# An attention and spectral-mixing kernel: the first two output pairs take the last two chunks of modes from their sums in place of one

## The chip, the cores and the metric

The kernel runs on one core of a Trainium2 chip. The core has five engines that run side by side, each with an instruction queue of its own that is worked off in order: TensorE (PE in the profile, with its weight loads as PEld), VectorE (DVE), ScalarE (ACT), GpSimd (POOL) and SyncE (SP). In this kernel POOL and SP do little but issue transfers (DMAs), which sixteen DMA engines carry out. Matrix products land in PSUM[...]; everything else lies in SBUF, 128 partitions wide.

The metric is the device time of one execution in microseconds. The time of a kernel is the median of several executions.

## The reference

First causal attention with a bias that decays, for 8 batches and 8 heads, over 576 positions with 64 numbers each. Its output, with the heads side by side, is `x` (8 x 576 x 512). Then a spectral layer:

```python
X = np.fft.rfft(x, axis=1)                 # 64 modes are kept
Xr, Xi = real(X[:, :64]), imag(X[:, :64])
Yr = einsum('bmd,mde->bme', Xr, w_r) - einsum('bmd,mde->bme', Xi, w_i)
Yi = einsum('bmd,mde->bme', Xr, w_i) + einsum('bmd,mde->bme', Xi, w_r)
y = np.fft.irfft(Yr + 1j * Yi, n=576, axis=1)
u = x + y
return u + np.maximum(u @ w_ch, 0.0)
```

`w_r` and `w_i` are 64 x 512 x 512 in float32, 64 MiB each, and each number of them is used once for all batches.

## The kernel before

**Stages.** The loop over `n` (32 steps, up to about 340 us) does attention for two heads of one batch at a time, and the forward Fourier sums (`fft`). The 512 columns of `x` come in four groups `g` of 128; the modes come in eight chunks `c` of eight. `modes(g, c)` multiplies one chunk with the weights of one group: 16 matmuls in four lots `x` = 0 to 3, each with one weight tile of its own (real and imaginary part, even and odd modes). The sums over the groups are kept in `y_acc`; the last group, `g` = NG - 1, gives the finished chunk `yb` (128 rows: 16 of real and imaginary modes for each of 8 batches, by 512 columns, float16).

**Weights.** POOL issues the loads (`load`, L217), 512 KB into each tile, into a ring of tiles. The issue of a load waits until `modes` has read the tile that it replaces. The loads for the last chunk are all issued by the time chunk 5 of the last group has been multiplied.

**After a chunk.** `spread` (L465) issues from SP a transfer inside SBUF that sorts the 16 x 8 rows of `yb` so that rows 16c to 16c+15 of `yv[:, b, 0, :]` hold chunk c for batch b. `y_transposed` and `y_times_wch` form `v = yb @ w_ch` (a cast `v_sb` on DVE at the end, L630), and a second `spread` puts it into `yv[:, b, 1, :]`.

**Outputs.** `pairs` lists the output tiles two by two: pair 0 is positions 0 to 255 of batch 0, pair 1 positions 256 to 511 of batch 0. For each, `u` = x + G.y (`start_u` L678, then `add_y` with `which` = 0, L659) and `z` = x @ w_ch + G.(y @ w_ch) (`add_y` with `which` = 1), where G are the numbers of the inverse transform. Then `relu` and `finish` (L712) give the result, and SP sends it out (L714). For pairs 2 and on the product x @ w_ch was formed earlier and kept (`keep`); pairs 0 and 1 (`NPRE` = 2) take it straight from PSUM (`x_transposed` L590, `x_times_wch` L600).

**The first two pairs.** So that they need not wait for the last chunk to be sorted, `add_y` reads only the first `GK` = 112 rows of `yv` for them (chunks 0 to 6), and `add_last` (L668) adds chunk 7 from `yb` or `vb` directly. Its stationary operand `Gx_sb` holds the 16 rows of G for chunk 7, at every eighth partition, and zeros elsewhere, so that of the 128 rows of `yb` only those of batch 0 count. It is loaded whole, zeros included, by one transfer from SP (L561).

**Order.** The order of each engine's instructions is that of the program text (`manual_schedule`); waits are put in by the framework wherever a tile is written and read. TensorE's order at the end of the chunks, L731 to L748, is written out by hand: `x_transposed(0)`, `x_transposed(1)`, `x_times_wch(0)`, `modes(3, 6)`, `y_transposed`, `y_times_wch(6)`, `x_times_wch(1)`, `start_u(0)`, `add_y` of u for pair 0, then `modes(3, 7)`, in which the call `meanwhile` ahead of lot 3 (L438) does `add_y` of z for pairs 0 and 1. L750 to L773 then finish pairs 0 and 1, and the loop at L802 does the other sixteen.

**PSUM.** Two slots each for the pools `aux` (chunk sums, transposes, v), `u` and `z`.

Of the kernel before, what the change touches and what calls it, by code (L numbers as in the profile page):

```python
# [9 lines left out]
FP32 = mybir.dt.float32  # L10
FP16 = mybir.dt.float16
# [7 lines left out]
def kernel(  # L19
# [11 lines left out]
    nc = tc.nc  # L31
    B, H, S, D = q.shape
    NM = moe_w_r.shape[0]
    DM = H * D
    P = 128
# [4 lines left out]
    NG = DM // P  # L40
# [5 lines left out]
    MC = 8  # L46
    NCK = NM // MC
# [3 lines left out]
    NF = NT - 1  # L51
# [10 lines left out]
        axis=1,  # L62
# [11 lines left out]
    G_np = np.zeros((NM, 2, SP), dtype=np.float64)  # L74
    G_np[:, 0, :S] = cmv[:, None] * np.cos(ang.T)
    G_np[:, 1, :S] = -(cmv[:, None] * np.sin(ang.T))
    G_np = G_np.reshape(P, SP).astype(np.float16)
# [6 lines left out]
    d_Ff = nc.inline_tensor(Ff_np, name="c_Ffwd").ap()  # L84
    d_G = nc.inline_tensor(G_np, name="c_Ginv").ap()

    Gx_np = np.zeros((2 * MC, B, NF * P), dtype=np.float16)
    Gx_np[:, 0] = G_np[-2 * MC :, : NF * P]
    d_Gx = nc.inline_tensor(Gx_np.reshape(P, NF * P), name="c_Ginvx").ap()

    ctx.enter_context(tc.manual_schedule())
    gp = ctx.enter_context(tc.tile_pool(name="globals", bufs=1))
# [98 lines left out]
    def ring_of(k):  # L191
        if k < NE:
            return None
        return int(k < LW2 and (k - NE) % (WA + WB) >= WA)
# [33 lines left out]
    for n in range(N):  # L228
# [3 lines left out]
        while nt < min(w, len(wq)):  # L232
            i = ring_of(nt)
# [37 lines left out]
    with tc.tile_pool(name="cum_psum", bufs=1, space=PSUM) as cpsum:  # L271
# [5 lines left out]
            out=cum, data0=spos, data1=zer, initial=0.0, op0=ALU.add, op1=ALU.add  # L277
# [16 lines left out]
        for x in range(2):  # L294
            rows = slice(NL * x, NL * x + NL)
            nc.vector.tensor_copy(
                out=cumt4[rows, :], in_=cumt_sb[rows, NK, x::2]
# [132 lines left out]
    def modes(g, c, meanwhile=None):  # L430


        ps = auxpool.tile([P, DM], FP32, name="yp", tag="aux")
        for x in range(4):
            ri, par = divmod(x, 2)
            cols = xs[g % 2].rearrange("p k r b m -> p (k r b) m")
            c0 = (48, 16)[ri] - 16 * par
            if x == 3 and meanwhile:  # L438
                meanwhile()
            for cg in range(4):  # L440
                nc.tensor.matmul(  # L441
                    ps[32 * cg : 32 * cg + 32, :],
                    cols[:, c0 : c0 + 32, c * MC + 2 * cg + par],
                    wt[(g, c, ri, par)][:, cg, :],
                    start=(x == 0), stop=(x == 3),
                    tile_position=(0, 32 * cg), skip_group_check=True,
                )
        if g == 0:
            nc.vector.tensor_copy(out=y_acc[:, c, :], in_=ps)
        elif g < NG - 1:  # L450
            nc.vector.tensor_tensor(out=y_acc[:, c, :], in0=ps, in1=y_acc[:, c, :], op=ALU.add)
        else:
            yb = spool.tile([P, DM], FP16, name="y_sb", tag="y")
            for cols in halves if c == NCK - 1 else [slice(0, DM)]:
                nc.vector.tensor_tensor(
                    out=yb[:, cols], in0=ps[:, cols], in1=y_acc[:, c, cols], op=ALU.add
                )
            spread(c, 0, yb)
            return yb
# [3 lines left out]
    def spread(c, which, rows):  # L463

        nc.sync.dma_start(out=yv[16 * c : 16 * c + 16, :, which, :], in_=rows)  # L465
# [7 lines left out]
    NPRE = 2  # L473
# [45 lines left out]
    with tc.tile_pool(name="sc_psum", bufs=2, space=PSUM) as scpool, \  # L519
# [7 lines left out]
        for n in range(N):  # L527
# [9 lines left out]
            i = first_pairs[n - N + len(first_pairs)] if n >= N - len(first_pairs) else None  # L537
# [19 lines left out]

    finpool = ctx.enter_context(tc.tile_pool(name="fin_sb", bufs=1))
    yv = finpool.tile([P, B, 2, DM], FP16, name="yv")
    Gx_sb = finpool.tile([P, NF * P], FP16, name="Gx_sb")  # L560
    nc.sync.dma_start(out=Gx_sb, in_=d_Gx)  # L561
    upool = ctx.enter_context(tc.tile_pool(name="u_psum", bufs=2, space=PSUM))
    zpool = ctx.enter_context(tc.tile_pool(name="z_psum", bufs=2, space=PSUM))

# [13 lines left out]
    def parts(b, T):  # L578

        if T < NF:  # L580
            return [(slice(0, P), b, ident16h)]
        return [(slice(NL * i, NL * i + NL), b + i, ident16h[:NL, :NL]) for i in range(2)]

    def x_transposed(i):
        xts[i] = xt_sb[len(xts) % 2]
        for x, (b, T) in enumerate(pairs[i]):
            ps = upool.tile([P, DT, P], FP32, name="xt_ps", tag="u")
            for rows, bb, ident in parts(b, T):
                for dt in range(DT):
                    nc.tensor.matmul(  # L590
                        ps[:, dt, rows], x_all[: rows.stop - rows.start, dt, bb, T, :],
                        ident, start=True, stop=True, skip_group_check=True,
                    )
            nc.vector.tensor_copy(out=xts[i][:, x], in_=ps)

    def x_times_wch(i, last):
        zs[i] = z = zpool.tile([P, 2, DM], FP32, name="z_ps", tag="z")
        for x in range(2):
            for dt in range(DT):
                nc.tensor.matmul(  # L600
                    z[:, x, :], xts[i][:, x, dt, :], wch_sb[:, dt, :],
                    start=(dt == 0), stop=(last and dt == DT - 1), skip_group_check=True,
                )
# [11 lines left out]
    def y_transposed(yb):  # L615
        ps = auxpool.tile([P, DT, P], FP16, name="yt_ps", tag="aux")
        for dt in range(DT):
            nc.tensor.transpose(ps[:, dt, :], yb[:, bass.ts(dt, P)], ident16h)
        yt = spool.tile([P, DT, P], FP16, name="yt_sb", tag="yt")
        nc.scalar.copy(out=yt, in_=ps)  # L620
        return yt

    def y_times_wch(c, yt):
        vp = auxpool.tile([P, DM], FP32, name="v_ps", tag="aux")
        for dt in range(DT):
            nc.tensor.matmul(
                vp, yt[:, dt, :], wch_sb[:, dt, :], start=(dt == 0), stop=(dt == DT - 1)
            )
        vb = spool.tile([P, DM], FP16, name="v_sb", tag="v")
        nc.vector.tensor_copy(out=vb, in_=vp)  # L630
        spread(c, 1, vb)
        return vb
# [17 lines left out]
    order_z = list(late)  # L650
    TAKE = (3, 2, 2, 2, 1, 0)
    us, rs = {}, {}
    GK = P - 2 * MC

    def add_y(dst, i, which, rows=slice(0, P), start=False):

        for x, (b, T) in enumerate(pairs[i]):
            for r, bb, _ in parts(b, T):
                nc.tensor.matmul(  # L659
                    dst[x][r, :], G_sb[rows, bass.ds(T * P, r.stop - r.start)],  # L660
                    yv[rows, bb, which, :], start=start, stop=True, skip_group_check=True,
                    tile_position=(0, r.start),
                )

    def add_last(dst, i, yb, cols=slice(0, DM)):

        for x, (b, T) in enumerate(pairs[i]):
            nc.tensor.matmul(  # L668
                dst[x][:, cols], Gx_sb[:, bass.ts(T, P)], yb[:, cols],
                start=False, stop=True, skip_group_check=True,  # L670
            )

    def start_u(i):
        pool, tag = ((upool, "u"), (auxpool, "aux"))[i % 2]
        us[i] = [pool.tile([P, DM], FP32, name="u_ps", tag=tag) for x in range(2)]
        for x, (b, T) in enumerate(pairs[i]):
            for r, bb, ident in parts(b, T):
                nc.tensor.matmul(  # L678
                    us[i][x][r, :].rearrange("p (g d) -> p g d", d=P), ident,
                    x_all[: r.stop - r.start, :, bb, T, :],  # L680
                    start=True, stop=False, skip_group_check=True, tile_position=(0, r.start),
                )
# [35 lines left out]
    def z_of(i):  # L718
        return [zs[i][:, x, :] for x in range(2)]

    for c in range(NCK - 2):
        yb = modes(NG - 1, c)
        for x in range(TAKE[c] - 1):
            work()
        yt = y_transposed(yb)
        if TAKE[c]:
            work()
        y_times_wch(c, yt)
    work()
    assert not order_z and not ahead  # L730
    c = NCK - 2  # L731
    for i in range(NPRE):
        x_transposed(i)
    x_times_wch(0, False)
    yb = modes(NG - 1, c)
    yt = y_transposed(yb)
    y_times_wch(c, yt)
    x_times_wch(1, False)


    start_u(0)
    add_y(us[0], 0, 0, slice(0, GK))

    def first_sums():
        for i in range(NPRE):
            add_y(z_of(i), i, 1, slice(0, GK))

    yb = modes(NG - 1, NCK - 1, first_sums)  # L748

    yt = spool.tile([P, DT, P], FP16, name="yt_sb", tag="yt")  # L750
    for x in range(2):
        dts = slice(x * DT // 2, (x + 1) * DT // 2)
        ps = auxpool.tile([P, DT // 2, P], FP16, name="yt_ps", tag="aux")
        for dt in range(dts.start, dts.stop):
            nc.tensor.transpose(ps[:, dt - dts.start, :], yb[:, bass.ts(dt, P)], ident16h)
        nc.scalar.copy(out=yt[:, dts], in_=ps)
    add_last(us[0], 0, yb)
    vb = spool.tile([P, DM], FP16, name="v_sb", tag="v")
    for cols in halves:
# [7 lines left out]
    for i in range(NPRE):  # L767
        for cols in halves:
            add_last(z_of(i), i, vb, cols)
        relu(i, 2 - i)  # L770
    start_u(1)
    add_y(us[1], 1, 0, slice(0, GK))
    add_last(us[1], 1, yb)  # L773


# [65 lines left out]
```

The softmax here doesn't subtract the row's maximum and nothing guards it: scores larger than these inputs give would overflow.

## Time and profile before

| | |
|---|---|
| median of 10 runs | 463.58 us (461.79 to 464.46) |
| profiled execution | 463.75 us, of which 462.0 us are the span of the profile |
| busy in the span | PE 343.6 us (74%), DVE 233.5 (51%), ACT 219.0 (47%), POOL 182.9 (40%) |
| DMA | 95.16 MB, 206 GB/s on the mean |
| POOL's queue of transfers (the weights among them) | 81.81 MB |
| weight loads (L217) | 512 KB each |
| landing of the sixteen `yv` spreads (128 KB each) | 2.9 to 6.5 us after issue, median 5.9 |
| load of `Gx_sb` (128 KB, L561) | issued at 340.34 us, landed 5.1 us later |
| first output transfer | issued at 428.58 us |

Times inside the profile are microseconds from the start of the span. "Busy" of a matmul runs from its start to its modelled end, and since matmuls overlap, single durations are longer than the spacing of a row of them. The profile also gives the share of full speed at which TensorE's clock ran.

### The profile page before, as it was taken

Reading aid. Unit: us, or ns where it says so; the run is one execution under the profiler, and the core shown is the slowest. Engines: PE = TensorE matmul, PEld = TensorE weight load, DVE = VectorE, ACT = ScalarE, POOL = GpSimd, SP = SyncE. Lnnn points to the kernel's source line nnn. Section 1 sums busy time; section 2 is a strip of 40 time slices with the busy share of each in tenths; the row PEclk is TensorE's granted clock in tenths of the full one; section 3 lists DMA queues with packets and bytes.
Section 4 is the critical chain, followed back from the end, with each engine's and each line's share of the span. In section 5 each row is a group of like instructions: output and inputs, shape, how many; then the busy total and the mean of one; then the engine's idle time right before and its main releaser. Section 6 shows DMA issues by size and latency. Waiting matters only on the chain.

```text
span 462.0 us, 10254 instructions
## 1 busy us (share of the span) xinstructions
PE 343.6 (74%) x4185; PEld 214.4 (46%) x4185; DVE 233.5 (51%) x523; ACT 219.0 (47%) x382; POOL 182.9 (40%) x269
## 2 busy tenths in 40 slices
PE   1879988956663989746398776889968675576995
PEld 1456666634442666434265544566644342233432
DVE  6775666643332657524265543476566342231675
ACT  1585885554342657623265443556603131110895
POOL 6755545534445455344454444445232222100000
PEclk9995999997776899958787988899989897797999
DMA  9999999999999999999999999999999999992687
GB/s 175 201 203 203 201 203 202 203 204 204 204 204 199 203 202 203 204 204 204 200 196 204 204 204 205 205 202 203 206 211 213 214 214 215 215 213 57 228 305 299
DMA packets 110063, 95.16 MB, mean 206 GB/s; under 512 B 28544, under 2 KB 105216, under 8 KB 110016
## 3 DMA queue, kind: packets, MB, share of 16 engines
q0 software_dynamic: 98960, 81.81, 111.8%
q1 hardware_dynamic: 11056, 12.70, 8.9%
q8 instruction: 33, 0.54, 0.4%
q14 instruction: 14, 0.11, 0.1%
HBM read 164.66 MB, written 9.44 MB: 377 GB/s over the span
## 4 chain that ended last, share of the span: by engine, by line
DMA 73%; PE 17%; issue 4%; POOL 3%; DVE 1%; DVEq 0%; ACT 0%; POOLq 0%; ACTq 0%
DMA w_sb<-in_moe_w_i_dram 33%; DMA q<-in_q_dram 15%; DMA w_sb<-in_moe_w_r_dram 12%; DMA k<-in_k_dram 4%; DMA x_all<-in_moe_w_r_dram 2%; DMA v<-in_v_dram 2%; PE z_ps L659 2%; PE sc_ps L365 2%; DMA y_acc<-in_moe_w_r_dram 2%; DMA y_acc<-in_moe_w_i_dram 2%; PE u_ps L659 2%; PE u_ps L678 2%; POOL w_sb L217 2%; PE yp L441 2%; PE tr_ps L324 1%
## 5 line engine op out<-in xcount | busy, mean ns | idle before, releaser
L373 ACT ACTIVATE p_sb<-sc_ps,cumt_sb 128x576 f16<-128x576 f32 (+1 forms) x256 | 141.8, 635 | 46.9 <-PE sc_ps L365 46.4
L217 POOL DMA_DIRECT2D w_sb<-in_moe_w_i_dram x60 | 45.0, 750 | 80.2 <-PE yp L441 33.7
L217 POOL DMA_DIRECT2D w_sb<-in_moe_w_r_dram x60 | 45.3, 756 | 69.0 <-DMA w_sb<-in_moe_w_r_dram 19.2
L217 POOL DMA_DIRECT2D v<-in_v_dram x72 | 50.7, 706 | 32.6 <-DMA w_sb<-in_moe_w_r_dram 8.8
L324 PE MATMUL tr_ps<-ident,q 64*64 64x64 bf16 x576 | 17.5, 210 | 52.6 <-DMA q<-in_q_dram 52.5
L441 PE MATMUL yp<-w_sb,xs 128*32 128x512 bf16 x480 | 38.9, 425 | 23.6 <-DMA w_sb<-in_moe_w_i_dram 19.5
L359 PE MATMUL sc_ps<-negm,ident 128*128 128x256 bf16 x256 | 55.8, 304 | 0.2
L327 DVE COPY qtA<-tr_ps 64x576 bf16<-64x576 bf16 x32 | 23.7, 741 | 48.7 <-PE tr_ps L324 48.7
L394 PE MATMUL av_ps<-v,p_sb 128*128 128x65 f16 x1024 | 44.5, 198 | 0.0
L344 ACT ACTIVATE p<-sc_ps,cumt 128x64 f16<-128x64 f32 x32 | 10.0, 314 | 72.5 <-PE sc_ps L340 72.4
L365 PE MATMUL sc_ps<-qtB,ktB 128*128 128x512 bf16 (+2 forms) x192 | 43.2, 341 | 0.0
L394 PEld LDWEIGHTS <-p_sb 128*128 128x128 f16 x1024 | 39.5, 100 | 4.9 <-issue 0.8
L327 DVE COPY ktA<-tr_ps 64x576 bf16<-64x576 bf16 x32 | 24.0, 749 | 32.1 <-PE tr_ps L324 32.1
L324 PEld LDWEIGHTS <-q 64*64 64x64 bf16 x576 | 13.6, 123 | 55.3 <-DMA q<-in_q_dram 54.2
L441 PEld LDWEIGHTS <-xs 128*32 128x32 bf16 x512 | 22.7, 170 | 35.5 <-issue 32.2
L365 PE MATMUL sc_ps<-qtA,ktA 65*128 65x512 bf16 (+2 forms) x192 | 37.3, 304 | 0.3 <-DVE ktA L327 0.3
L399 DVE TENSOR_REDUCE den<-av_ps 128x5 f32<-128x10 f32 x64 | 10.8, 169 | 49.1 <-PE av_ps L394 49.1
L404 DVE TENSOR_TENSOR x_all<-av_ps,rcp 128x320 f16<-128x320 f32 x64 | 31.5, 491 | 2.2
L327 ACT COPY ktB<-tr_ps 64x576 bf16<-64x576 bf16 x32 | 20.3, 633 | 20.5 <-DVE ktA L327 19.4
L365 PEld LDWEIGHTS <-ktB 128*128 128x128 bf16 x192 | 22.1, 115 | 14.5 <-issue 5.9
L324 PE MATMUL tr_ps<-ident,k 64*64 64x64 bf16 x576 | 17.1, 208 | 15.5 <-DVE qtB L327 10.1
L600 PE MATMUL z_ps<-wch_sb,xs 128*128 128x512 f16 x96 | 26.8, 429 | 0.0
(106 smaller groups left out, 517.3 us busy)
## 6 DMA issues: line engine op xcount, KB each, us to landing
w_sb<-in_moe_w_r_dram POOLq DMA_DIRECT2D x60, 512.0 KB, 12.0
w_sb<-in_moe_w_i_dram POOLq DMA_DIRECT2D x60, 512.0 KB, 11.9
q<-in_q_dram POOLq DMA_DIRECT2D x32, 144.0 KB, 9.7
k<-in_k_dram POOLq DMA_DIRECT2D x32, 144.0 KB, 10.0
v<-in_v_dram POOLq DMA_DIRECT2D x72, 64.0 KB, 9.7
out_dram<-r_sb SPq DMA_DIRECT2D x16, 256.0 KB, 2.4
out_dram<-r_w SPq DMA_DIRECT2D x16, 256.0 KB, 2.4
x_all<-in_moe_w_i_dram POOLq DMA_DIRECT2D x3, 512.0 KB, 10.2
```

What stands on the lines that cost most here:

```text
L217: nc.gpsimd.dma_start(out=dst, in_=src)
L324: nc.tensor.transpose(ps[rows, r, :], src[rows, r, :], ident16[rows, rows])
L327: copy(out=dst[n % NQ][rows, :].rearrange("d (p r) -> d p r", r=R), in_=ps[rows].rearrange("d r p -> d p r"),)
L359: nc.tensor.matmul(ps[:, bass.ds(w * S, W)], ident16, negm[:, bass.ts(r, W)], start=True, stop=False, skip_group_check=True,)
L365: nc.tensor.matmul(ps[:, c0 : c0 + i1 - i0], keys[:, w, r, :], qt[:, i0:i1], start=False, stop=True, skip_group_check=True,)
L373: nc.scalar.activation(out=pt[:, poff[x] : poff[x] + S - w * W], in_=ps[:, w * S : (w + 1) * S - w * W], func=ACTF.Exp, bias=cumt_sb[:, x, ...
L394: nc.tensor.matmul(ps[:, I, r : r + NCH], lhsT, rhs, start=(i == 0), stop=(i == len(todo) - 1), skip_group_check=True,)
L399: nc.vector.tensor_reduce(out=den, in_=ps[:, :, 0 : VW : NCH], axis=mybir.AxisListType.X, op=ALU.add)
L404: nc.vector.tensor_tensor(out=x_all[:, g, b, :, D * h : D * h + D], in0=ps[:, :, 1 : NCH], in1=rcp.unsqueeze(2).to_broadcast([P, NT, D]), ...
L441: nc.tensor.matmul(ps[32 * cg : 32 * cg + 32, :], cols[:, c0 : c0 + 32, c * MC + 2 * cg + par], wt[(g, c, ri, par)][:, cg, :], start=(x == ...
L600: nc.tensor.matmul(z[:, x, :], xts[i][:, x, dt, :], wch_sb[:, dt, :], start=(dt == 0), stop=(last and dt == DT - 1), skip_group_check=True,)
L659: nc.tensor.matmul(dst[x][r, :], G_sb[rows, bass.ds(T * P, r.stop - r.start)], yv[rows, bb, which, :], start=start, stop=True, skip_group_ ...
```

## The change

`Gx_sb` becomes two tables, for chunks 6 and 7; it is set to zero by a memset on DVE, and only the 16 partitions with numbers in them are loaded. `GK` falls from 112 to 96: `add_y` for pairs 0 and 1 now reads chunks 0 to 5, and `add_last` is called twice for each sum, for chunk 6 (`c=0`) with `yb6` or `vb6` and for chunk 7. The order on TensorE changes: `x_transposed(1)` comes after `modes(3, 6)`, `x_times_wch(1)` ahead of `y_times_wch(6)`; the start of u for pair 0 moves into `modes(3, 7)` ahead of lot 2, and z of both pairs stays ahead of lot 3.

```diff
-    Gx_np = np.zeros((2 * MC, B, NF * P), dtype=np.float16)
-    Gx_np[:, 0] = G_np[-2 * MC :, : NF * P]
-    d_Gx = nc.inline_tensor(Gx_np.reshape(P, NF * P), name="c_Ginvx").ap()
+    NX = 2
+    Gx_np = np.stack([G_np[2 * MC * c :, : NF * P][: 2 * MC] for c in range(NCK - NX, NCK)], axis=1)
+    d_Gx = nc.inline_tensor(np.ascontiguousarray(Gx_np), name="c_Ginvx").ap()
...
-            if x == 3 and meanwhile:
-                meanwhile()
+            if meanwhile and x in meanwhile:
+                meanwhile[x]()
...
-    Gx_sb = finpool.tile([P, NF * P], FP16, name="Gx_sb")
-    nc.sync.dma_start(out=Gx_sb, in_=d_Gx)
+    Gx_sb = finpool.tile([P, NX, NF * P], FP16, name="Gx_sb")
+    nc.vector.memset(Gx_sb.rearrange("p c t -> p (c t)").bitcast(FP32), 0.0)
+    nc.sync.dma_start(out=Gx_sb[0:P:B], in_=d_Gx)
...
-    GK = P - 2 * MC
+    GK = P - 2 * MC * NX
...
-    def add_last(dst, i, yb, cols=slice(0, DM)):
+    def add_last(dst, i, yb, cols=slice(0, DM), c=NX - 1):
...
-                dst[x][:, cols], Gx_sb[:, bass.ts(T, P)], yb[:, cols],
+                dst[x][:, cols], Gx_sb[:, c, bass.ts(T, P)], yb[:, cols],
...
     c = NCK - 2
-    for i in range(NPRE):
-        x_transposed(i)
+    x_transposed(0)
     x_times_wch(0, False)
-    yb = modes(NG - 1, c)
-    yt = y_transposed(yb)
-    y_times_wch(c, yt)
+    yb6 = modes(NG - 1, c)
+    x_transposed(1)
+    yt = y_transposed(yb6)
     x_times_wch(1, False)
-    start_u(0)
-    add_y(us[0], 0, 0, slice(0, GK))
-
-    def first_sums():
+    vb6 = y_times_wch(c, yt)
+
+    def first_u():
+        start_u(0)
+        add_y(us[0], 0, 0, slice(0, GK))
+        add_last(us[0], 0, yb6, c=0)
+
+    def first_z():
         for i in range(NPRE):
             add_y(z_of(i), i, 1, slice(0, GK))
-
-    yb = modes(NG - 1, NCK - 1, first_sums)
+            add_last(z_of(i), i, vb6, c=0)
+
+    yb = modes(NG - 1, NCK - 1, {2: first_u, 3: first_z})
...
     start_u(1)
     add_y(us[1], 1, 0, slice(0, GK))
+    add_last(us[1], 1, yb6, c=0)
     add_last(us[1], 1, yb)
```

## The prediction

> **What bounds the kernel now.** I read the chain of waits first, in order of time. Up to 397.74 us it is made of weight loads: one lands, a chunk is multiplied, POOL may issue the next. From 427 us to 456.87 it is TensorE alone, and the windows of 5 us from 430 to 455 each show PE busy 5.00 of 5.00: whatever reaches 427 earlier ends earlier by as much, and each matmul added there costs its full time. The change lies between, where the chain says (start, length, what):
>
> ```profile
> 376.22 21.52 DMA w_sb<-in_moe_w_i_dram
> 397.74 0.04 issue
> 397.79 0.48 PE yp L441 x4
> ...
> 410.58 0.70 DVE y_sb L455
> 411.28 0.02 issue
> 411.30 6.20 DMA yv<-y_sb
> 417.49 0.05 issue
> 417.54 0.60 PE u_ps L659 x2
> 418.14 0.83 PE yp L441 x9
> 418.98 1.03 issue
> 420.01 1.87 PE z_ps L659 x4
> 421.88 0.64 PE yp L441 x4
> ```
>
> PE stops twice: from 415.65 (end of `start_u`) to 417.54 for the spread of chunk 6's y, and for 1.03 us ahead of `add_y` of z. "Issue" hides a transfer there: the spread of chunk 6's v was issued at 414.25 and took 5.7 us, so it landed at 419.95. The change takes both waits away, 1.89 + 1.03 = 2.92 us.
>
> **What is late next.** Lot 3 of the last chunk needs the last weight tile. At the tile `w_sb` the trace shows its issue:
>
> ```profile
> L217 POOL DMA_DIRECT2D w_sb<-in_moe_w_i_dram x1: 740/740/740, 398.3 to 398.3; - x1
> ...
> DMA to landing us min/median/max: 21.9/21.9/21.9
> ```
>
> 398.27 + 21.9 = 420.17. The DMA windows agree: the rate falls to nothing at 419.8. In the same way lot 2's tile lands at 395.76 + 22.0 = 417.76, lot 1's at 393.42 + 20.8 = 414.2, and lot 3's of chunk 6 at 387.23 + 22.0 = 409.23. None of these issues moves, for they come before the reordered part. So lot 3, which began at 421.81, can begin at 420.22 at best: of 2.92 us, 1.59 are to be had. The rest becomes a wait for weights.
>
> **Part by part.**
>
> **1. The new order.** From the rows: a 128x512 matmul takes 0.216 us at full clock and 0.43 at half (1.73 and 3.41 for eight). After 405.46 PE has `x_transposed(0)` (0.7), `x_times_wch(0)` behind its casts (done at 407.3; ends about 408.5), chunk 6, whose lot 3 lands at 409.23 (ends 409.5; the sum on DVE, 0.69, ends 410.2). `x_transposed(1)` now fills that wait; its two casts queue on DVE behind the sum and end at 411.5. `x_times_wch(1)` runs 411.0 to 412.7, `y_times_wch` to 413.6. The later v cast (0.69) has its spread issued at about 414.3, where it was; landing near 420, first used by pair 2 near 428. Lots 0 and 1 end at 414.5, held by the landing at 414.2. Then `start_u`, `add_y` and the new `add_last`, six matmuls, 1.3: 415.8. PE waits there for lot 2 until 417.81, so the reordering and the two added u matmuls cost nothing, with 1.9 us of cover. After lot 2 (0.3) come eight z matmuls, four of them new: 418.1 to 419.85 at full clock, still under the landing at 420.17. That cover is only 0.3 us, and at half clock it is gone.
>
> **2. Two more matmuls in u of pair 1.** They stand where PE never stops: 2 x 0.216 = +0.43. The spread of the last v (issued 426.80, 2.9 to land, wanted at 429.76) hid nothing that this could use: PE and landing came together.
>
> **3. Fewer rows.** Matmuls over 96 rows for 112: the row with 112 (0.60 for two) equals that with 128 (0.59). Nothing.
>
> **4. Memset and load.** 128 x 512 float32; the row of 128x2560 took 2.19, so 0.44 by size. It sits on DVE between the last Fourier copies (end 341.97) and the first sum (343.34), where DVE is idle for 1.37. If it waits for memory of the attention stage, the sum, and behind it casts and PE, wait too; but the old load of the same tile went at 340.34, so the memory is free by then. Taken at zero, ends 0 and, as in the slower case below, several us. The load shrinks from 128 to 32 KB: at 207 GB/s between 0 and -0.46; taken as 0, since the stream then also waits for PE's reads.
>
> **5. The clock.** The windows below are cut at the instants at which the clock changes, 3.41 us apart (columns: span, length, busy PE, PEld, DVE, ACT, POOL with counts, PE clock, DMA share, GB/s):
>
> ```profile
> 351.10:354.51 3.41, 1.58 (x25) 1.04 (x22) 2.18 (x3) 0.08 (x1) 1.11 (x2) 1.00 1.24 208
> ...
> 412.54:415.95 3.41, 3.11 (x14) 1.20 (x14) 0.69 (x1) 0.00 (x0) 0.00 (x0) 1.00 1.22 218
> 415.95:419.37 3.42, 1.44 (x14) 0.56 (x14) 0.00 (x0) 0.00 (x0) 0.00 (x0) 1.00 0.73 129
> 419.37:422.78 3.41, 2.47 (x8) 0.61 (x8) 0.24 (x1) 0.00 (x0) 0.00 (x0) 0.50 0.05 7
> 422.78:426.19 3.41, 3.17 (x15) 1.93 (x16) 0.94 (x3) 0.65 (x2) 0.00 (x0) 0.50 0.16 43
> 426.19:429.61 3.42, 3.14 (x19) 1.71 (x18) 2.05 (x4) 2.34 (x4) 0.00 (x0) 1.00 0.19 59
> ```
>
> A window with PE 42% busy was followed by half clock; 72% did not bring it back, 93% did; the window at 351.10 with 46% kept it. So the stretch from lot 3 to the last v cast, all of the critical tail, ran at half clock. In the changed kernel the window from 415.95 holds PE work from 417.81 on, 1.56 us or 46%: on the edge. Here a rule of the Trainium skill speaks ("TensorE: Matmul & The Clock Gate", "Why this matters for your kernels": "No PE-idle gaps >~3µs between matmul bursts"). By it neither kernel drops, as the longest gap is 1.9 us; the row at 415.95 shows a drop after gaps of 1.6 and 0.4 within the window, so the trace decides. The sums by each:
>
> - Rule, full clock: lot 3 ends at 420.22 + 0.48 = 420.70 for 422.49, -1.79. From the last y sum to the last v cast (422.54 to 426.82, 4.28) PE's pieces are transposes 0.72, u 0.85, v 1.72. At full clock v starts 1.43 after the sum (second half of the sum, 0.2 of transposes, 0.43 of u), v takes 0.87, the cast 0.5: 2.80, so -1.48. With +0.43: **-2.84**.
> - Row, half clock at 419.37: of eight z matmuls 5.7 are done, 2.3 x 0.43 remain, lot 3 runs 420.36 to 421.0: -1.45. The window to 422.78 is then busy 84% (idle only for the y sum), between the 72% and 93% seen. If the clock returns at 422.78, v saves 0.85: -1.45 - 0.85 + 0.43 = **-1.87**. If at 426.19, the z sums ahead of `relu` run partly at half clock (+0.32): -1.45 + 0.32 + 0.43 = **-0.70**.
>
> **The sum.** The profiled execution was 463.75 us, 462.0 of span and 1.75 outside that nothing here touches; it stands 0.17 above the median 463.58, and I apply the differences to the median. The clock's instants do not follow the kernel's start in anything that one profile shows, so the runs may mix these cases. I take the row, between its ends: -1.29, **462.3 us**, own range 461.7 to 462.9.
>
> **The rivals.**
>
> - **Full clock kept** (460.7 us). For it: 46% was enough at 351.10, and the second gap shrinks from 1.03 to 0.3. Against: 0.02 us decides. Chance 0.32, with 0.42 for the forecast.
> - **The wait moves, nothing is gained** (463.7 us, 463.2 to 464.1). If the clock's instant falls about 1.6 us sooner, at 417.8, the window before it holds the whole 1.9 us gap, 41% busy. Lot 2 and the eight z matmuls then run at half: 418.45 + 3.44 = 421.89, later than the 421.81 of before. With 0.43 for u: +0.5; less if the busy stretch brings the clock back a window sooner (-0.85). The mean is near +0.1. Chance 0.14.
> - **It doesn't do what it says; slower** (465.7 us). If a wait for `yv` is counted by tile and not by rows, `add_y` over rows 0 to 95 still waits for chunk 6's rows. z then starts at 420.0, now with eight matmuls, 3.44 at half clock, where four took 1.87: +1.6, and +0.43: +2.1. At full clock it would be about +0.4 at most, so half clock is where it turns. Against it: VectorE writes rows 64 to 127 of `qtB` while a transfer to row 0 of the same kind of tile is under way, with no wait on either:
>
> ```profile
> 311.67 0.50 SPq L311 DMA_DIRECT2D qtA<-ncum_sb  x1
> 311.98 0.76 DVE L327 COPY qtB<-tr_ps 64x576 bf16<-64x576 bf16 x1
> 312.37 0.50 SPq L312 DMA_DIRECT2D qtB<-ncum_sb  x1
> ```
>
> The transfer into `qtB` is issued 0.37 us before that copy has ended. Chance 0.06.
> - **The memset blocks DVE; slower** (near 466 us). Were it held by a transfer into its memory for 5 to 6 us (the landings of that time), DVE would be late by 5.5 - 0.9 = 4.6; PE's reads, and with them the issue of weights, would follow: -1.3 + 4.6. It decides from a hold beyond 0.9 us. Against it is the old load at 340.34. Chance 0.06.
>
> **Chances.** Differences under 0.2%, 0.93 us, can't be told from none; faster is below 462.65, slower above 464.5. Faster: 0.32 and about 0.30 of the forecast's 0.42, 0.62. Same: 0.12 + 0.14 = 0.26. Slower: 0.12. The range goes from full clock with some of the smaller load's gain (460.4) to the top of the third case (464.1), leaving out the slower two.
>
> **What would show it.** In the chain: no `yv` transfer between 405 and 425, a weight load that ends at about 420.2 ahead of lot 3, and before it a gap of some 1.9 us ahead of lot 2. In the windows: whether the clock after 419 is 1.00 or 0.50. At the last y sum: start near 420.8 for 422.54. Pair 1: six matmuls in u for four. The memset: near 0.44 us, before 343.3, with `y_sb` of chunk 0 not later. I am wrong if lot 3 starts much before 420.2 (then the weights landed earlier, and the stream had slack that I don't see), or if PE still stands ahead of `add_y`.

## The result, and the profile after

The changed kernel takes 460.18 us in the median (14 runs, 459.97 to 461.51), the kernel before 463.61 us (51 runs, 460.18 to 465.89). The ratio is 0.9936, with a 95% interval of 0.9919 to 0.9953: 3.0 us less, 2.2 to 3.8. The profiled execution took 459.97 us with a span of 458.2. Not only the median fell: the runs of the changed kernel lie within 1.5 us, those of before within 5.7, and the middle half of them within 0.6 us for 1.8.

The chain of waits of the changed kernel, in the stretch that answers to the one shown of before:

```profile
397.51 22.12 DMA w_sb<-in_moe_w_i_dram
419.63 0.04 issue
419.67 0.48 PE yp L441 x4
420.15 0.02 issue
420.18 0.44 DVE y_sb L455
...
422.62 0.43 DVE v_sb L769
423.05 0.04 issue
423.09 0.81 PE z_ps L669 x6
423.91 0.43 PE u_ps L679 x2
424.34 0.43 PE u_ps L660 x2
424.77 0.86 PE u_ps L669 x4
425.64 0.86 PE z_ps L789 x4
```

No spread is left in it. The last weight tile lands at 419.63 and lot 3 begins 0.04 us later. From the start of the last y sum to the first z matmul behind the last v cast the chain takes 2.91 us (420.18 to 423.09) where it took 4.28 (422.54 to 426.82). The added matmuls of u for pair 1 stand in the line of 0.86 us. The timeline shows the two new waits, both for weights, and that `add_y` over 96 rows of y ran while chunk 6's spread was still on its way (issued at 409.79, 5.9 us to land):

```profile
344.27 0.48 DVE L561 MEMSET Gx_sb<- 128x512 f32 x1 [0.45 <-DVE xs L425]
...
409.79 0.55 SPq L465 DMA_DIRECT2D yv<-y_sb  x1
...
414.39 0.60 PE L660 MATMUL u_ps<-yv,G_sb 96*128 96x512 f16 x2
...
416.64 0.46 PE L441 MATMUL yp<-w_sb,xs 128*32 128x512 bf16 x4 [1.23 <-DMA w_sb<-in_moe_w_i_dram]
...
419.67 0.46 PE L441 MATMUL yp<-w_sb,xs 128*32 128x512 bf16 x4 [0.73 <-DMA w_sb<-in_moe_w_i_dram]
```

And the windows, cut again at the instants at which this execution's clock changes (columns as in the prediction; the number after POOL's count is the clock):

```profile
413.76:417.17 3.41, 2.18 (x15) 0.91 (x12) 0.15 (x1) 0.00 (x0) 0.00 (x0) 1.00 1.03 195
417.17:420.59 3.42, 2.23 (x12) 0.87 (x10) 0.41 (x2) 0.00 (x0) 0.00 (x0) 1.00 0.29 55
420.59:424.00 3.41, 3.16 (x24) 2.04 (x25) 1.19 (x4) 1.14 (x3) 0.00 (x0) 1.00 0.15 43
```

The clock stays at 1.00. The two windows that hold the waits are 64% and 65% busy; the one that counted before was 42%.

**Where the time came from.** Between the two spans lie 3.8 us. Lot 3 begins 2.14 us earlier (419.67 for 421.81). From there to the y sum it is 0.22 shorter, and the chain behind it 1.37. The stretch from the last v cast to the start of z of pair 2 (L789, in the kernel before L784) is 0.43 longer (2.55 for 2.12). The rest, 0.5, falls in the outputs; the last transfers landed after 2.1 us for 2.4. Of the 2.14 us, 0.54 is an earlier landing of the last weights. The four z matmuls of before took 1.80 us from their start to lot 3, and four take 0.87 at full clock, so 0.93 is clock and the other 0.67 is waiting. By this account the clock gives 2.5 us, the removed waits 0.7, and the added matmuls take 0.43. The account is read from two executions; the runs below try whether the clock is the cause.

### The profile page after: what moved, and what is told of

Read it like the earlier page. It is cut to its first block, busy times and chain, and to the rows that moved or that the text cites. A ratio compares the mean times of both kernels' runs of the same rounds, so it can differ in the third digit from the quotient of the medians.

```text
span 458.2 us, 10271 instructions
## 1 busy us (share of the span) xinstructions
PE 343.5 (75%) x4193; PEld 215.2 (47%) x4193; DVE 233.8 (51%) x524; ACT 219.1 (48%) x382; POOL 183.0 (40%) x269
## 4 chain that ended last, share of the span: by engine, by line
DMA 67%; PE 22%; DVE 3%; POOL 3%; issue 2%; ACT 1%; DVEq 0%; POOLq 0%; ACTq 0%
DMA w_sb<-in_moe_w_i_dram 36%; DMA q<-in_q_dram 10%; DMA w_sb<-in_moe_w_r_dram 7%; DMA v<-in_v_dram 6%; DMA x_all<-in_moe_w_i_dram 4%; PE yp L441 3%; PE sc_ps L365 2%; DMA k<-in_k_dram 2%; PE av_ps L394 2%; DMA y_acc<-in_moe_w_r_dram 2%; PE sc_ps L359 2%; PE u_ps L679 2%; PE z_ps L660 2%; PE tr_ps L324 2%; PE u_ps L660 2%
## 5 line engine op out<-in xcount | busy, mean ns | idle before, releaser
L217 POOL DMA_DIRECT2D w_sb<-in_moe_w_i_dram x60 | 45.1, 751 | 82.4 <-PE yp L441 39.9
L441 PE MATMUL yp<-w_sb,xs 128*32 128x512 bf16 x480 | 37.0, 407 | 24.1 <-DMA w_sb<-in_moe_w_i_dram 20.0
L365 PE MATMUL sc_ps<-qtB,ktB 128*128 128x512 bf16 (+2 forms) x192 | 44.9, 352 | 0.0
```

What stands on the lines that cost most here:

```text
L217: nc.gpsimd.dma_start(out=dst, in_=src)
L365: nc.tensor.matmul(ps[:, c0 : c0 + i1 - i0], keys[:, w, r, :], qt[:, i0:i1], start=False, stop=True, skip_group_check=True,)
L441: nc.tensor.matmul(ps[32 * cg : 32 * cg + 32, :], cols[:, c0 : c0 + 32, c * MC + 2 * cg + par], wt[(g, c, ri, par)][:, cg, :], start=(x == ...
```

## The experiments

**The clock alone, in the kernel before.** If the clock is what pays, matmuls that compute nothing of use should bring most of the gain with both waits still there. First one wait is filled:

```diff
     def start_u(i, fill=0):
...
+        for _ in range(fill):
+            nc.tensor.matmul(us[i][0], ident16h, G_sb[:, :DM], start=True, stop=True, ...)
...
-    start_u(0)
+    start_u(0, 8)
```

> The kernel before with eight more matmuls (8 x 0.216 = 1.73 us) into the PSUM tile of u, ahead of the start of u of pair 0, where TensorE stood for 1.9 us; their result is overwritten, and both waits for the spreads stay. Theory 1 (the gain is two parts: lot 3 begins earlier, and the clock stays at full): the clock alone is tried here. Lot 3 then begins at 420.0 + 0.87 = 420.9 for 421.8, ends 0.2 sooner in itself, and the chain to the last v cast takes 2.9 us for 4.3: about -2.5 where the clock had fallen, so near 461.2, with most runs close together, and clock 1.00 after 419. Theory 2 (the removed waits are the gain, the clock is secondary): within 0.5 us of the kernel before, since both waits are still there.

Measured: 461.88 us (460.46 to 463.3), ratio 0.9969 (0.9950 to 0.9988). About half of the gain, with nothing but idle matmuls added, so theory 2 falls; but theory 1 had promised more. The windows of its profiled execution say why: the clock held past the first wait, now filled, and fell at the second (1.32 us ahead of z).

```profile
418.29:421.70 3.41, 1.69 (x10) 0.61 (x10) 0.75 (x2) 0.00 (x0) 0.00 (x0) 0.99 0.22 42
421.70:425.11 3.41, 3.37 (x15) 2.02 (x15) 0.79 (x3) 0.74 (x2) 0.00 (x0) 0.51 0.13 38
```

The first is 50% busy as it is cut here; the clock changes 0.07 us before its end, and the 3.41 us up to that instant are 48% busy. The next window runs at half clock. So both waits were filled, the second with matmuls that add zeros to u:

```diff
     def first_sums():
+        for _ in range(6):
+            nc.tensor.matmul(us[0][0], ident16h, zrow, start=False, stop=True, ...)
```

> The kernel before with both waits for the spreads filled: eight matmuls ahead of the start of u of pair 0 (overwritten), and six that add zeros to that sum ahead of z (6 x 0.216 = 1.3 us, the length of the second wait). Both waits stay. Theory 1 (clock): full clock to the end, lot 3 at the landing of v (about 420.0) + 0.87 = 420.9, 0.7 later than the last weights, and no added matmuls in u of pair 1 (-0.43): 0.3 us above the changed kernel, near 460.5, with a spread of about 1 us. Theory 2 (the removed waits are the gain): the first filling alone gave 461.9; a second one gives nothing more, 461.9 or later.

Measured: 460.72 us (460.15 to 462.1), ratio 0.9941 (0.9915 to 0.9966); the changed kernel has 0.9936. Its chain of waits, and the window that holds the second wait:

```profile
417.94 1.40 PE u_ps L750 x6
419.34 0.88 PE z_ps L661 x4
420.23 0.47 PE yp L441 x4
420.72 0.44 DVE y_sb L455
```

```profile
417.35:420.77 3.42, 3.32 (x26) 1.24 (x18) 0.05 (x1) 0.00 (x0) 0.00 (x0) 1.00 0.42 80
```

The six useless matmuls cover the wait for v's spread, z follows in 0.88, and lot 3 begins at 420.23. The last weights of this execution landed at 398.22 + 22.0 = 420.22. So at full clock the waits for the spreads cost nothing here: by the time that they end, the weights have only just come. This kernel is also spared the two matmuls that the change adds to u of pair 1 (0.43 us). That filling alone brings what the change brings is the main result of the study.

**The clock taken from the changed kernel.** The reverse: same matmuls, same removed waits, but the two waits for weights made one.

```diff
-    yb = modes(NG - 1, NCK - 1, {2: first_u, 3: first_z})
+    yb = modes(NG - 1, NCK - 1, {2: lambda: (first_u(), first_z())})
```

> The changed kernel with its eight z matmuls moved from ahead of lot 3 to ahead of lot 2, behind those of u: the same matmuls, the same waits removed, lot 3 still at the landing of the last weights, but TensorE's two waits (1.2 and 0.7 us in the profile) become one of about 2.3 us. Theory 1 (clock): a window of 3.41 us that holds all or most of this wait is under 46% busy, so in about half of the runs the clock falls, which costs 1.3 us to the last v cast: median about 461 and a wide spread (460.0 to 462). Theory 2 (waits only): 460.2, as the changed kernel.

Measured: 462.13 us (460.07 to 463.46, 22 runs), ratio 0.9950 (0.9936 to 0.9964). That interval overlaps with the changed kernel's (0.9919 to 0.9953), so the ratio alone does not show a loss; the wide scatter and the trace do. The windows of its profiled execution, which took 462.54:

```profile
414.67:418.09 3.42, 3.38 (x21) 1.47 (x22) 0.69 (x1) 0.00 (x0) 0.00 (x0) 1.00 1.11 208
418.09:421.50 3.41, 1.43 (x11) 0.46 (x9) 0.00 (x0) 0.00 (x0) 0.00 (x0) 1.00 0.26 55
421.50:424.91 3.41, 2.90 (x14) 1.68 (x15) 1.18 (x3) 0.65 (x2) 0.00 (x0) 0.50 0.16 43
424.91:428.33 3.42, 3.12 (x20) 1.78 (x19) 1.92 (x4) 2.21 (x4) 0.00 (x0) 1.00 0.14 43
```

One window with 42% busy, and the next, which holds the chain of y and v, runs at half. TensorE stood 1.96 us ahead of lot 3, which began at the landing (420.99 and 0.04), so no wait for a spread came back. Then the hole was filled with eight matmuls that add zeros to half of the rows of u, by a stationary operand from the zero columns of `G_sb` past position 576:

```diff
+    def fill():
+        for _ in range(8):
+            nc.tensor.matmul(us[0][0][0:RP, :], G_sb[:, S:SP], wch_sb[:, 0, :], start=False, stop=True, ...)
...
-    yb = modes(NG - 1, NCK - 1, {2: lambda: (first_u(), first_z())})
+    yb = modes(NG - 1, NCK - 1, {2: lambda: (first_u(), first_z()), 3: fill})
```

> The changed kernel with z ahead of lot 2 (the run that gave 462.1), and with eight matmuls that add zeros to half of the rows of a sum in the wait that opened ahead of lot 3 (8 x 0.216 = 1.73 of 2.3 us). Theory 1 (clock): back to the changed kernel, 460.2 to 460.6, and a narrow spread. Theory 2 (moving z costs by its order): stays at 462.

Measured: 461.22 us (460.51 to 461.96), ratio 0.9923 (0.9903 to 0.9942), and the clock at 1.00 through the stretch. In the same session the changed kernel was run again:

> The changed kernel itself, to have it on the same chip as the others. Both theories: ratio to the kernel before of 0.992 to 0.995.

Measured: 460.91 us, ratio 0.9918 (0.9898 to 0.9938), just under what was expected. The kernel before stood at 464.94 in that session, so ratios are to be compared, not medians. Filled, the kernel with z moved is not told apart from the changed kernel (0.9923 and 0.9918): once the clock is kept, no cost of the order is left to see.

**The new order alone.** The sums of chunk 6 come from the spread again, and with them the single table, loaded whole; order and late start of u are those of the change.

```diff
-    NX = 2
+    NX = 1
...
-        add_last(us[0], 0, yb6, c=0)
...
-            add_last(z_of(i), i, vb6, c=0)
...
-    add_last(us[1], 1, yb6, c=0)
```

> The changed kernel with the sums of chunk 6 taken from the spread again (112 rows, one table, dense load, the added matmuls left out of u and z): the new order alone. u waits for the spread of y of chunk 6, landing near 416 and hidden under lot 2's weights; z of both pairs waits for the spread of v, landing near 419.7, then 0.87: lot 3 at 420.6 to 420.9 for 419.7. Theory 1 (clock): TensorE stands from about 418 to 419.7 and for shorter times before, a window falls under 46% in many runs, and the time is 461 to 463, clearly slower than the changed kernel although it saves 0.43 us in u of pair 1. Theory 2 (waits only): +0.9 - 0.43, so about 0.5 us slower than the changed kernel, 460.7, and close together.

Measured: 465.0 us (464.25 to 466.02), ratio 1.0027 (1.0013 to 1.0041): slower than the kernel before, and by 2 us slower than even theory 1 had said. The windows show most of the reason:

```profile
414.89:418.30 3.41, 1.85 (x12) 0.51 (x8) 0.57 (x1) 0.00 (x0) 0.00 (x0) 1.00 1.04 194
418.30:421.71 3.41, 1.51 (x7) 0.48 (x7) 0.00 (x0) 0.00 (x0) 0.00 (x0) 0.50 0.28 55
421.71:425.13 3.42, 2.88 (x13) 0.90 (x12) 0.76 (x2) 0.65 (x2) 0.00 (x0) 0.50 0.02 5
```

Three waits in a row (1.15, 0.64 and 1.66 us: y's spread, weights, v's spread) take two windows to 54% and 44%, and the third, with 84%, does not bring the clock back: half from 418.3 to 428.5, three windows where before had two. In this execution the last outputs also took 3.3 us to land for 2.4 before. That it is the clock was tried with five and six idle matmuls in two of the waits:

> The new order alone (as in the run that gave 465.0), with TensorE's waits filled: five matmuls ahead of the start of u of pair 0 (overwritten) and six that add zeros to it ahead of z. Theory 1 (that run was slow by its clock, at half from 418.4 to 428.6): full clock to the end, z at the landing of v's spread plus 0.87, 0.5 to 0.7 us later than the last weights, minus 0.43 in u of pair 1: near 460.7, over 4 us less from work that computes nothing. Theory 2 (the order itself, or the wait for v's spread, makes it slow): 464 or more.

Measured: 461.85 us (461.09 to 463.14) beside 464.94, ratio 0.9938 (0.9917 to 0.9958), with the clock at 1.00 from 405 to the last output. Eleven matmuls that compute nothing take about 4 us out of this kernel (1.0027 to 0.9938). Against the 463.61 of before the ratio means 460.7, as expected.

**Filling the changed kernel.** Five idle matmuls in its wait ahead of lot 2:

> The changed kernel with five more matmuls (1.08 us) in the wait ahead of lot 2, overwritten later. Theory 1: the clock is kept already in most runs, so the median stays within 0.2 us of the changed kernel; only the upper runs (461.1, 461.5) could come down. Theory 2: the same median. If the changed kernel still lost clock in half of its runs, it gains 0.5 us or more here.

Measured: 460.84 us, ratio 0.9943 (0.9920 to 0.9966), no different from the changed kernel's. It kept its clock already.

**The smaller load.** The memset and the load of 16 partitions alone, in the kernel before:

```diff
-    nc.sync.dma_start(out=Gx_sb, in_=d_Gx)
+    nc.vector.memset(Gx_sb.bitcast(FP32), 0.0)
+    nc.sync.dma_start(out=Gx_sb[0:P:B], in_=d_Gx)
```

> The kernel before with only the load of the table for chunk 7 changed: memset on DVE, then 16 partitions loaded (16 KB for 128 KB). Theory A (the smaller load lets the stream of weights land 0.5 us sooner, 419.63 for 420.17 in the two profiles): last landing near 419.7, and up to -0.5 us, about 463.1. Theory B (the difference of landings is that of two executions): landing anywhere between 419.6 and 420.6, time within 0.3 us of the kernel before, as the kernel before does not wait for that landing anyway.

Measured: 462.91 us (459.87 to 465.48), ratio 0.9989 (0.9969 to 1.0009), last weights at 420.04, 0.13 us from before: no difference that can be told, so nothing ties the 0.54 between the two first profiles to the smaller load. Over the fourteen profiles of this study that landing lies between 419.6 and 421.3. The two kernels that were profiled twice repeat theirs within 0.2 (419.63 and 419.85; 420.28 and 420.45), so the landing may differ by program and not only by execution; that was not settled.

The profiled execution of this run also shows what luck does. Both waits for the spreads are in it (1.62 and 1.35 us), but the clock's windows divide the idle time between them and the clock is kept:

```profile
413.94:417.35 3.41, 1.79 (x14) 0.72 (x16) 0.00 (x0) 0.00 (x0) 0.00 (x0) 1.00 1.17 215
417.35:420.77 3.42, 1.88 (x20) 0.52 (x12) 0.14 (x1) 0.00 (x0) 0.00 (x0) 1.00 0.39 75
```

They are 52% and 55% busy. Cut 0.8 us later, the first would have been 42% busy, as in the profile before. This execution took 460.10 us, and the 38.3 us from landing to the end of the span are as good as the changed kernel's.

**The price of the added matmuls in u of pair 1.** They can go, since chunk 6's rows have landed long before:

```diff
-    add_y(us[1], 1, 0, slice(0, GK))
-    add_last(us[1], 1, yb6, c=0)
+    add_y(us[1], 1, 0, slice(0, P - 2 * MC))
```

> The changed kernel with u of pair 1 reading 112 rows of the spread, as before the change, so that its two added matmuls go; chunk 6's rows landed about 8 us earlier. Theory 1: 2 x 0.216 us of a TensorE that never stops, so 0.43 us faster than the changed kernel, 459.7; the spread of the last v, wanted 0.43 us sooner, lands at about the same moment. Theory 2 (that spread binds as soon as TensorE comes earlier): 0 to 0.1 us.

Measured: 460.93 us, ratio 0.9940 (0.9912 to 0.9968): the 0.43 us that were expected don't show. And with all 128 rows from the spread, `add_last` for pair 1 gone:

> The changed kernel with u of pair 1 reading all 128 rows of the spread: four matmuls go, 0.86 us. Chunk 7's y was issued at 420.96 and takes 3.1 us, landing at 424.06; it is read at 424.2. Theory 1: z of pair 2 would come at 425.64, but the spread of v of chunk 7 (423.07 + 2.9) lands at 425.97, so 0.33 us turn into a wait: 0.5 us faster than the changed kernel, 459.7. Theory 2: landing after the read also in u, so less than e5 gains.

Measured: 460.51 us, ratio 0.9923 (0.9894 to 0.9952), with 0.34 us of waiting for v's spread, as expected. Its interval holds the changed kernel's 0.9936. Once more beside the changed kernel:

> The changed kernel with u of pair 1 from all 128 rows of the spread, once more, beside the changed kernel on the same chip. If the four matmuls that go count in full less the wait of 0.34 us that the profile showed: 0.5 us under the changed kernel. If the end is set elsewhere: 0.0 to 0.2 us.

Measured: 460.82 us, ratio 0.9915 (0.9897 to 0.9932), the changed kernel 0.9918. Not told apart. From the landing of the last weights to TensorE's last matmul it is 0.3 us shorter (33.5 for 33.8), but the last output transfers took 2.4 us to land where they took 2.1; in all three profiles of the two kernels with fewer matmuls in u the median is 2.4 to 2.6. Whether that is their doing or chance was not settled. No version that is clearly faster than the changed kernel was found.

| profiled execution | last weights land, us | clock behind lot 3 | end of the span minus landing, us |
|---|---|---|---|
| before | 420.2 | 0.50 | 41.8 |
| before, one wait filled | 420.1 | 0.50 for a window | 39.9 |
| before, both filled | 420.2 | 1.00 | 38.2 |
| changed | 419.6 | 1.00 | 38.6 |
| changed, again | 419.8 | 1.00 | 38.6 |
| changed, z ahead of lot 2 | 421.0 | 0.50 for a window | 39.8 |
| the same, filled | 421.0 | 1.00 | 38.6 |
| order alone | 421.1 | 0.50 | 42.9 |
| order alone, filled | 421.3 | 1.00 | 38.9 |

The rows with full clock end 38.2 to 38.9 us after the landing, whether the kernel waits for spreads or not; those with half clock behind lot 3 end 39.8 to 42.9 us after it.

## Why the prediction was right and wrong

- **The bound** was named rightly: of the removed 2.92 us of waiting only what lies before the landing of the last weights is gained, and lot 3 now begins 0.04 us after it.
- **The likeliest case fell, and the first rival came.** The forecast was 462.3 us with the clock at half for part of the stretch; "full clock kept" stood at 460.7 with a chance of 0.32. Measured are 460.18, or 460.6 by the ratio applied to 463.58. The median lies 0.2 below the low end of the range, the ratio's value inside it. That the range reaches down so far is due to its having been drawn to take in the rival; the mechanism that was chosen did not come about.
- **The step that failed** is the size of one wait in the clock's part. The prediction put TensorE at lot 2 at 415.8 and its weights at 417.76, a wait of 1.9 us and a window 46% busy, "on the edge". Measured: 415.4 and about 416.6, a wait of 1.23. Lot 2's landing had been taken from one execution. It came 2.4 us ahead of lot 3's there and 3.0 in the profile after; over the fourteen profiles the lead is 2.4 to 3.0, so the one used was at the end of them. With 1.23 and 0.73 us of waiting, 3 us apart, no window of 3.41 us in this stretch of the profile after is under 61% busy, at whatever instant it is cut. This fits with the runs lying so close together. "On the edge" was a fair reading of 46%: in the fourteen profiles windows from 44% to 54% lost the clock in some places and kept it in others.
- **The sum for full clock** held: -2.84 predicted against -3.0 by the ratio (2.2 to 3.8). The chain behind the y sum took 2.91 us for 2.80, the added matmuls of u +0.43 as said. Two matmuls over 96 rows took the 0.60 of two over 112, and the smaller load brought nothing that can be told. Some of the agreement is chance: in the profile after, 0.54 us come from an earlier landing that the sum had not taken in.
- **Rule against row.** The rule quoted in the prediction, against idle gaps over about 3 us, would have given the right case here, but not for its reason. With z ahead of lot 2 TensorE stood 1.96 us, less than 3, and the clock fell; in this stretch of the kernel before it fell with no gap over 1.9 us. How busy the whole window was fits these cases better, though near half it does not decide.
- **The memset** took 0.48 us for 0.44 and the y sum followed on its heels at 344.85, when its matmuls had just ended, so it was not held up. **The wait by tile**, the slower rival, is excluded by the 96-row `add_y` at 414.39, since the spread landed at about 415.7.
- **What the prediction had not seen**: how much the clock alone is worth. Its sum for full clock credits the chain behind the y sum with 1.48 us, but it never asked what full clock would bring with the waits left in. With both waits filled and nothing else changed the kernel before reaches 0.9941, where the change reaches 0.9936.

## What to carry to other kernels

Before a short wait of TensorE is removed, ask what the clock does after it. A wait that hides behind a later transfer can still cost time through half clock on the chain behind; here fourteen matmuls of no use, put into two such waits, were worth as much as the whole change. Sum TensorE's busy time over windows of the clock's period (3.41 us here), at every place that the windows can have, and spread the waits that can't be avoided so that none of these windows falls to about half. Where the runs of a kernel scatter by over 1% with the same work, look whether chance decides this in it.

## What the runs showed of the hardware

- The clock changes on a grid of 3.41 us whose place against the kernel differs between executions (it came back to full at 405.73 us in the profile before, at 403.50 in the one after).
- From 340 us on, over the fourteen profiles, every window of this grid under 44% busy was followed by half clock and none from 55% up; from 44% to 54% either happened. Earlier, in the attention loop, windows of up to 64% were followed by half clock, so the share of busy time is not the whole of it.
- At half clock in the same stretch, all windows from 88% up brought the clock back; from 78% to 87% some did (85% with z ahead of lot 2, as cut above) and some did not (84% with the order alone).
- Matmuls that add zeros, 128 rows by 128 or by 64 columns, hold the clock: with them the windows of the waits were 97% busy and kept it (both waits filled; z ahead of lot 2, filled).
- The last output transfers landed after 2.0 to 2.6 us, once after 3.3 (the order alone), and the end of the span moves with them by up to 1.2 us. The cause is open.
